# One loop for the score and value products, weights per unit, one eviction per block, in an attention kernel on one core

## The chip, the core and the metric

The kernel runs on one core of a Trainium2 chip. The core has five engines that run side by side, each with its own instruction stream: TensorE (PE in the profile; its weight loads are listed apart, as PEld), VectorE (DVE), ScalarE (ACT), GpSimd (POOL) and SyncE (SP), which here only issues transfers. Transfers between the main memory (DRAM) and the on-chip memory (SBUF) run on 16 DMA engines; matrix products go to the accumulator memory (PSUM). The engines wait for each other on semaphores. The metric is the device time of one execution in microseconds (us), lower is better.

## What is computed

Attention for 128 heads (8 batches of 16) with 16 queries per head, 2048 keys, head size 256, all bf16:

```python
B, H, Sq, Skv, Dh = 8, 16, 16, 2048, 256
def reference(q, k, v):
    scale = q.shape[-1] ** -0.5
    scores = jnp.einsum('bhqd,bhkd->bhqk', q, k) * scale
    attn = _softmax(scores, axis=-1)
    return jnp.einsum('bhqk,bhkd->bhqd', attn, v)
```

K and V are 134 MB each and every byte is read once; q and the output are 1 MB each.

## The kernel before

**Units and blocks.** The 128 heads are cut into 16 blocks of 8 heads (`g`, 0 to 15, `last` is 15), each block into two units of 4 heads (`e`, 0 and 1). K or V of one unit is 4.19 MB and fills one of four SBUF slots of `SL`: `KA` and `KB` for K of unit 0 and 1, `VA` and `VB` for V. K of block 0 goes to the V slots instead (`kslot`, L93), so that K of block 1 can be loaded at once. K(g,e) and V(g,e) stand below for these transfers. A partition holds 64 consecutive rows (`T`) of the unit; t counts them.

**One block on the engines.** VectorE transposes K of a unit in place, in 32x32 squares of 4-byte words, in four instructions of 16 rows each (L154); each pair of them releases one half `h` of the unit's scores (`c_kt[e][h]`). TensorE then makes the scores of both units into four PSUM banks `S_ps` (`qk`, L239 to L247): for each of 8 weight sets, 2 products per half, one weight load for each pair (L233 leaves the load out for the second). The last product of a unit adds to `c_qk[e]`. VectorE takes the negated row maximum (L156), ScalarE the exponentials with their sums in two halves (L206), VectorE transposes them into `PTc` (L162), and ScalarE copies them with eight instructions into `PTz` (L219), the zero-padded weights of the second product. TensorE multiplies `PTz` with V, 64 rows t per unit, 128 products with 128 weight loads per block (`pv`, L249, L251), into one PSUM bank per unit (`obank`). ScalarE evicts each unit's rows with the factor 1/sum into `O_fin` (L180) and issues the store (L184); the products of block g-1 come behind the scores of block g, and so do their eviction and store (`finish`).

**TensorE's order.** Scores of block 0; then a loop over g = 1 to 15 of scores of g and products of g-1 (L266 to L274); then the products of block 15 written out, with their own weights (`z` = 1), their own two banks and a wait for each piece of V(15,0) (`TAIL_A`) and V(15,1) (`TAIL`, pieces of 19 down to 2 rows).

**Transfers.** SyncE issues all loads from one queue, in a fixed order, and a wait in it holds up all behind it (L99 to L134): q, K(0,0), K(0,1), then for each g K(g,0), K(g,1), V(g-1,0), V(g-1,1). K(g,e) waits for the scores that used the slot (`c_qk[e]`), V(g-1,e) for the products that used it (`c_pv[e]`). At the end V(15,0) and V(15,1) go to the K slots and wait for the scores of block 15 (L126 to L131). K(15,1) and V(14,1) are loaded in two halves, with a semaphore for each.

**ScalarE's order.** For block g: the next block's query weights (L174), the exponentials, then `finish(g-1)`, which waits for all products of g-1, and only then the eight copies into `PTz`, since one set of weights serves all blocks but the last.

Of the kernel before, what the change touches and what calls it, by code (L numbers as in the profile page):

```python
# [9 lines left out]
F32 = mybir.dt.float32  # L10
# [5 lines left out]
def bass_standalone__softmax_full_bidir__sampling_kernel(  # L16
# [20 lines left out]
    with ExitStack() as es:  # L37
# [5 lines left out]
        PTc = ec(nc.sbuf_tensor("PTc", [128, T, 32], BF16))  # L43
        PTz = ec(nc.sbuf_tensor("PTz", [128, 2, T, 128], BF16))
        O_fin = ec(nc.sbuf_tensor("O_fin", [128, 2, D], BF16))
# [6 lines left out]
        O_ps = ec(nc.psum_tensor("O_ps", [128, 4, 512], F32))  # L52
# [8 lines left out]
        s_st = [sem("s_st%d" % i) for i in range(2)]  # L61
# [12 lines left out]
        c_pl = sem("c_pl")  # L74
# [8 lines left out]
        TAIL = [(0, 19), (19, 14), (33, 10), (43, 7), (50, 5), (55, 4), (59, 3), (62, 2)]  # L83
        TAIL_A = [(0, 37), (37, 27)]
        s_tail = [sem("s_t%d" % i) for i in range(len(TAIL))]
        s_vl = [sem("s_vl%d" % i) for i in range(len(TAIL_A))]
        s_vc = sem("s_vc")
        s_kl = sem("s_kl")

        def obank(g, e):  # L90
            return e + (2 if g == last else 0)
# [7 lines left out]
        def on_sync(eng):  # L99
            eng.dma_start(QT[:], qh).then_inc(s_q, 16)  # L100
            for e in range(2):
                load(eng, ku, 0, e, kslot(0, e), 0, T, s_k0[e])
            for g in range(1, G):
                for e in range(2):
                    if g >= 2:
                        eng.wait_ge(c_qk[e], g)
                    if (g, e) != (last, 1):
                        load(eng, ku, g, e, kslot(g, e), 0, T, s_k[e])
                    else:
                        load(eng, ku, g, e, kslot(g, e), 0, 32, s_k[e])  # L110
                        load(eng, ku, g, e, kslot(g, e), 32, 32, s_kl)
                w = g - 1
                for e in range(2):
                    if w:
                        eng.wait_ge(c_pv[e], w)
                    else:
                        eng.wait_ge(c_qk[e], 1)
                    if (w, e) != (last - 1, 1):
                        load(eng, vu, w, e, (VA, VB)[e], 0, T, s_v[e])
                        if e:  # L120
                            eng.sem_inc(s_vc, 16)
                    else:
                        load(eng, vu, w, e, VB, 0, 32, s_v[e])
                        load(eng, vu, w, e, VB, 32, 32, s_vc)
# [7 lines left out]
            eng.wait_ge(c_ev, 2 * last + 2)  # L132
            eng.dma_start(oh[128 * last:128 * last + 128, :], O_fin[:, last % 2, :]).then_inc(s_fin, 16)
            eng.wait_ge(s_fin, 16)  # L134
# [4 lines left out]
        def on_vector(eng):  # L139
# [4 lines left out]
            for g in range(G):  # L144
                for e in range(2):
                    for c in range(4):
                        if g == 0 and c == 0:
                            eng.wait_ge(s_k0[e], 16)
                        elif c == 0:
                            eng.wait_ge(s_k[e], 16 * g)  # L150
                        elif (g, e, c) == (last, 1, 2):
                            eng.wait_ge(s_kl, 16)
                        x = SLf[:, kslot(g, e), 16 * c:16 * c + 16, :].rearrange("p t i -> p (t i)")
                        eng.transpose(x, x).then_inc(c_kt[e][c // 2], 1)  # L154
# [13 lines left out]
        def on_scalar(eng):  # L168
# [9 lines left out]
            def evac(g, e):  # L178
                rows = slice(64 * e, 64 * e + 64)
                eng.activation(O_fin[rows, g % 2, :], O_ps[rows, obank(g, e), 0:D],  # L180
                               ACTF.Copy, scale=rinv[rows, g:g + 1]).then_inc(c_ev, 1)

            def store(g):
                eng.dma_start(oh[128 * g:128 * g + 128, :], O_fin[:, g % 2, :]).then_inc(s_st[g % 2], 16)  # L184

            def finish(g):
                eng.wait_ge(c_ri, 2 * g + 2)
                if g >= 2:
                    eng.wait_ge(s_st[g % 2], 16 * (g // 2))
                for e in range(2):  # L190
                    eng.wait_ge(c_pv[e], g + 1)
                    evac(g, e)
                eng.wait_ge(c_ev, 2 * g + 2)
                store(g)
# [3 lines left out]
            for g in range(G):  # L198
                if g < last:
                    eng.wait_ge(c_qk[1], g + 1)  # L200
                    qwb(g + 1)
                eng.wait_ge(c_mx, g + 1)
                if g:
                    eng.wait_ge(c_pt, 2 * g)
# [9 lines left out]
                z = 1 if g == last else 0  # L214
                for e in range(2):
                    for a in range(4):
                        rs = 32 * (2 * e + a // 2)
                        sv = PTc[rs:rs + 32, :, :]
                        eng.activation(PTz[32 * a:32 * a + 32, z, :, 64 * e + 16 * a:64 * e + 16 * a + 16],  # L219
                                       sv[:, :, 16 * (a % 2):16 * (a % 2) + 16], ACTF.Copy).then_inc(c_cp, 1)  # L220
            finish(last - 1)
            eng.wait_ge(c_ri, 2 * G)
            eng.wait_ge(s_st[last % 2], 16 * (last // 2))
            eng.wait_ge(c_pl, 1)
            evac(last, 0)
            eng.wait_ge(c_pl, 2)
            evac(last, 1)
            eng.wait_ge(s_st[0], 16 * (G // 2))

        def on_tensor(eng):  # L230
# [8 lines left out]
            def qk(g, e, h, slot):  # L239
                kb0 = SL[:, slot, 0, :]  # L240
                for bp in range(8):
                    b, par = bp // 2, bp % 2
                    for c in (2 * h, 2 * h + 1):
                        ins = mm(S_ps[:, c, :], QW[:, e, :, bp],
                                 ap_of(kb0, kb0.offset + 16 * c * D + 64 * b + par, [[D, 16], [2, 32]]),
                                 e == 0 and bp == 0, e == 1 and bp == 7, c % 2 == 0)
                return ins  # L247

            def pv(e, slot, z, bank, t0, t1):  # L249
                for t in range(t0, t1):  # L250
                    ins = eng.matmul(O_ps[:, bank, 0:D], PTz[:, z, t, :], SL[:, slot, t, :],  # L251
                                     start=(t == 0), stop=(t == T - 1))
                return ins

            def qks(g):
                for e in range(2):
                    for h in range(2):
                        eng.wait_ge(c_kt[e][h], 2 * g + 2)
                        if e == 0 and h == 0 and not (isinstance(g, int) and g == 0):
                            eng.wait_ge(c_ex[1], g)  # L260
                        ins = qk(g, e, h, kslot(0, e) if isinstance(g, int) and g == 0 else (KA, KB)[e])
                    ins.then_inc(c_qk[e], 1)

            eng.wait_ge(c_qw, 4)
            qks(0)
            with nc.Fori(1, G, engines=[PE], head_slot={PE: 0}) as g:  # L266
                qks(g)
                eng.wait_ge(c_cp, 8 * g)
                for e in range(2):
                    eng.wait_ge(s_v[e], 16 * g)  # L270
                    if e:
                        pv(e, VB, 0, e, 0, 32)
                        eng.wait_ge(s_vc, 16 * g)
                    pv(e, (VA, VB)[e], 0, e, 32 * e, T).then_inc(c_pv[e], 1)  # L274
            eng.wait_ge(c_cp, 8 * G)
            for (a, n), s in zip(TAIL_A, s_vl):
                eng.wait_ge(s, 16)
                ins = pv(0, KA, 1, obank(last, 0), a, a + n)
            ins.then_inc(c_pl, 1)
            for (a, n), s in zip(TAIL, s_tail):  # L280
                eng.wait_ge(s, 16)
                ins = pv(1, KB, 1, obank(last, 1), a, a + n)
            ins.then_inc(c_pl, 1)
# [34 lines left out]
```

## Time and profile before

| | us |
|---|---|
| median of 3 runs (lowest to highest) | 636.06 (636.02 to 636.25) |
| the profiled execution | 636.1 |
| its span, first to last instruction | 634.8 |
| TensorE products busy | 488.3 |
| VectorE busy | 365.2 |
| ScalarE busy | 214.8 |

Busy times of different engines overlap. In the profile a row such as `L154 DVE STREAM_TRANSPOSE SL<-SL` names the line of the kernel, the engine, the operation, and the tile written and read. A row of the timeline has the start and the length in us; several like instructions are merged (x8), and square brackets give the engine's idle time before them and what ended it. SPq and ACTq are the issue of a transfer, not the transfer; how long one takes from issue to landing is told in rows of their own, with its size in KB.

### The profile page before, as it was taken

The page shows a single profiled execution, that of the slowest core. Times are in us where ns is not written, and L with a number is a line of the kernel's source. Part 1 is how long each engine was busy: PE and PEld are TensorE (multiplying, and loading weights), DVE is VectorE, ACT ScalarE, POOL GpSimd, SP SyncE. Part 2 cuts the span into 40 slices and gives each one's busy share as a digit, 9 for nine tenths or more (in the row PEclk, how much of TensorE's full clock was granted, in tenths as well). Part 3 has the DMA queues.
Part 4 walks back from the last instruction along what each step waited for, and adds up shares of the span by engine and source line. Part 5 has one row for each costly group of instructions (what it writes and reads, how often), then busy time and mean ns, then how long its engine had stood idle before and what let it go on. Part 6 is the DMA issues. An engine that isn't in the chain of part 4 may idle for free.

```text
span 634.8 us, 6396 instructions
## 1 busy us (share of the span) xinstructions
PE 488.3 (77%) x3072; PEld 274.9 (43%) x2560; DVE 365.2 (58%) x210; ACT 214.8 (34%) x289; POOL 7.1 (1%) x5
## 2 busy tenths in 40 slices
PE   0738989595896958869597795967959689595998
PEld 0202828154271532716336262452724527144287
DVE  2968583763738546294562945739366393663830
ACT  1042252525035250342513325142252322524170
POOL 4000000000000000000000000000000000000000
PEclk9978999798997989969799797998979989798899
DMA  8999999999999999999999999999999999999997
GB/s 376 436 441 432 428 432 432 430 430 431 432 429 434 429 432 433 429 434 429 433 430 429 432 429 433 430 430 433 434 429 436 433 433 432 432 432 425 430 425 285
DMA packets 13113, 270.64 MB, mean 426 GB/s; under 512 B 1456, under 2 KB 3760, under 8 KB 4400
## 3 DMA queue, kind: packets, MB, share of 16 engines
q1 hardware_dynamic: 10944, 269.55, 98.8%
q10 hardware_dynamic: 2160, 0.98, 0.5%
q8 instruction: 3, 0.05, 0.0%
q14 instruction: 6, 0.05, 0.0%
HBM read 269.48 MB, written 1.05 MB: 426 GB/s over the span
## 4 chain that ended last, share of the span: by engine, by line
DMA 58%; PE 23%; DVE 16%; ACT 2%; issue 0%; SPq 0%
DMA SL<-in_k_dram 58%; DVE SL L154 15%; PE S_ps L234 11%; PE S_ps L235 10%; PE O_ps L251 2%; ACT PTz L219 1%; DVE PTc L162 1%; DVE negm L156 1%; ACT P_sb L206 0%; ACT O_fin L180 0%; SPq L97 0%; SPq L100 0%; DVE rinv L166 0%; DVE ltot L164 0%
## 5 line engine op out<-in xcount | busy, mean ns | idle before, releaser
L154 DVE STREAM_TRANSPOSE SL<-SL 128x2048 f32<-128x2048 f32 x128 | 284.2, 2279 | 157.9 <-DMA SL<-in_k_dram 157.9
L234 PE MATMUL S_ps<-SL,QW 128*128 128x512 bf16 x512 | 214.0, 418 | 143.5 <-DVE SL L154 143.3
L251 PE MATMUL O_ps<-SL,PTz 128*128 128x256 bf16 x2048 | 226.3, 273 | 0.9 <-ACT PTz L219 0.7
L234 PEld LDWEIGHTS S_ps<-SL,QW 128*128 128x128 bf16 x512 | 75.1, 147 | 326.6 <-issue 171.7
L251 PEld LDWEIGHTS O_ps<-SL,PTz 128*128 128x128 bf16 x2048 | 199.8, 98 | 30.9 <-issue 4.5
L235 PE MATMUL S_ps<-SL,QW 128*128 128x512 bf16 x512 | 212.5, 415 | 0.0
L219 ACT ACTIVATE PTz<-PTc 32x1024 bf16<-32x1024 bf16 x128 | 134.9, 1054 | 11.3 <-ACT O_fin L180 5.9
L174 ACT ACTIVATE QW<-QT 32x256 bf16<-32x256 bf16 x64 | 26.8, 419 | 243.3 <-PE S_ps L235 236.2
L156 DVE TENSOR_REDUCE negm<-S_ps 128x1 f32<-128x2048 f32 x16 | 36.7, 2292 | 61.4 <-PE S_ps L235 61.4
L180 ACT ACTIVATE O_fin<-O_ps,rinv 64x256 bf16<-64x256 f32 x32 | 15.0, 468 | 137.6 <-PE O_ps L251 137.5
L162 DVE STREAM_TRANSPOSE PTc<-P_sb 128x1024 bf16<-128x1024 bf16 x32 | 37.9, 1224 | 20.3 <-ACT P_sb L206 20.3
L206 ACT ACTIVATE P_sb<-S_ps,negm 128x1024 bf16<-128x1024 f32 x32 | 35.3, 1109 | 25.5 <-DVE negm L156 25.5
L137 POOL MEMSET PTz<- 128x8192 f32 x1 | 6.9, 6924 | 0.3 <-POOLq L303 0.3
L206 ACT ACTIVATION_READ_ACCUMULATOR P_sb<-S_ps,negm 128x1 f32 x32 | 6.3, 196 | 0.0
L143 DVE STREAM_TRANSPOSE QT<-QT 128x2048 f32<-128x2048 f32 x1 | 2.3, 2312 | 3.7 <-DMA QT<-in_q_dram 3.7
L166 DVE RECIPROCAL rinv<-ltot 128x1 f32<-128x1 f32 x16 | 2.6, 164 | 0.5
L164 DVE TENSOR_REDUCE ltot<-lsum 128x1 f32<-128x2 f32 x16 | 1.8, 112 | 0.0
L174 ACT ACT_TABLE_LOAD x1 | 1.3, 1283 | 0.7 <-PEq L303 0.7
L140 DVE MEMSET QW<- 128x1024 f32 x1 | 0.9, 912 | 1.0 <-PEq L303 1.0
L303 POOL MEMSET const-bfloat16-1.0<- 128x1 bf16 x1 | 0.1, 101 | 0.0
L303 POOL MEMSET const-uint8-127<- 128x1 uint8 x1 | 0.1, 101 | 0.0
L303 POOL MEMSET const-float32-0.0<- 128x1 f32 x1 | 0.1, 98 | 0.2 <-issue 0.2
(1 smaller groups left out, 0.1 us busy)
## 6 DMA issues: line engine op xcount, KB each, us to landing
SL<-in_k_dram SPq DMA_DIRECT2D x31, 4096.0 KB, 25.8
SL<-in_v_dram SPq DMA_DIRECT2D x29, 4096.0 KB, 29.1
SL<-in_k_dram SPq DMA_DIRECT2D x2, 2048.0 KB, 23.7
SL<-in_v_dram SPq DMA_DIRECT2D x2, 2048.0 KB, 29.2
SL<-in_v_dram SPq DMA_DIRECT2D x1, 2368.0 KB, 21.6
SL<-in_v_dram SPq DMA_DIRECT2D x1, 1728.0 KB, 25.4
SL<-in_v_dram SPq DMA_DIRECT2D x1, 1216.0 KB, 20.7
QT<-in_q_dram SPq DMA_DIRECT2D x1, 1024.0 KB, 4.9
```

Source lines behind the costliest of these rows:

```text
L137: eng.memset(PTz[:].rearrange("p a t c -> p (a t c)").bitcast(F32), 0.0).then_inc(c_pool, 1)
L154: eng.transpose(x, x).then_inc(c_kt[e][c // 2], 1)
L156: eng.tensor_reduce(out=negm[:, g:g + 1], in_=S_ps[:].rearrange("p c n -> p (c n)"), axis=AX.X, op=ALU.max, negate=True).then_inc(c_mx, 1)
L162: eng.transpose(PTc[:, 32 * h:32 * h + 32, :].rearrange("p t x -> p (t x)"), P_sb[:, 1024 * h:1024 * h + 1024]).then_inc(c_pt, 1)
L166: eng.reciprocal(rinv[:, g:g + 1], ltot[:, g:g + 1]).then_inc(c_ri, 1)
L174: eng.activation(ap_of(dv, dv.offset, [[1024 + 512, 2], [2, 64], [1, 2]]), ap_of(sv, sv.offset + 2 * (8 * r + a), [[8, 2], [64, 64], [1, 2]]),
L180: eng.activation(O_fin[rows, g % 2, :], O_ps[rows, obank(g, e), 0:D], ACTF.Copy, scale=rinv[rows, g:g + 1]).then_inc(c_ev, 1)
L206: eng.activation(P_sb[:, 1024 * h:1024 * h + 1024], S_ps[:, 2 * h:2 * h + 2, :].rearrange("p c n -> p (c n)"), ACTF.Exp, bias=negm[:, g:g ...
L219: eng.activation(PTz[32 * a:32 * a + 32, z, :, 64 * e + 16 * a:64 * e + 16 * a + 16], sv[:, :, 16 * (a % 2):16 * (a % 2) + 16], ACTF.Copy) ...
L234: return eng.matmul(dst, w, x, start=start, stop=stop)
L235: return eng.add_instruction(mybir.InstMatmult(name=nc.get_next_instruction_name(), engine=PE, start_tensor_calc=start, stop_tensor_calc=stop,
L251: ins = eng.matmul(O_ps[:, bank, 0:D], PTz[:, z, t, :], SL[:, slot, t, :], start=(t == 0), stop=(t == T - 1))
```

## The change

TensorE's code outside the loop shrinks to the scores of block 0, which now wait for the whole transposed unit and take the four banks with one weight load for each of the 8 weight sets. The loop runs 16 passes, r = 1 to 16: scores of block r if r is below 16, then the products of block r-1, the last block's too. The piecewise waits for V stand in every pass, against a limit that is 1 up to the pass where the piece's own semaphore is really used; SyncE adds 1 to these semaphores once, at g = 1, to `c_ev` as well.

`PTz`'s two sets are now one per unit: copies of unit 0 fill set 0, columns 0 to 63, and those of unit 1 fill set 1, columns 64 to 127. All 128 products of a block add into one PSUM bank, which one instruction evicts. The first product of a block waits for the eviction of the block before (`c_ev`). Copies of unit 0 wait for unit 0's products of the block before, then comes that block's eviction and store, then the copies of unit 1. `O_fin` has a place for each block, and the waits for a free place go.

V of block 15 is loaded into `VA` and `VB`, behind the products of block 14, in the same pieces as before. K(15,0) is loaded in halves as K(15,1) was. V(14,1) is cut at row 33 instead of 32. VectorE transposes 32 rows per instruction instead of 16.

```diff
+        PIECES = [[(0, 37), (37, 27)],
+                  [(0, 19), (19, 14), (33, 10), (43, 7), (50, 5), (55, 4), (59, 3), (62, 2)]]
+        MID = 33
...
-                    if (g, e) != (last, 1):
+                    if g < last:
                         load(eng, ku, g, e, kslot(g, e), 0, T, s_k[e])
                     else:
                         load(eng, ku, g, e, kslot(g, e), 0, 32, s_k[e])
-                        load(eng, ku, g, e, kslot(g, e), 32, 32, s_kl)
...
-            eng.wait_ge(c_qk[0], G)
-            for (a, n), s in zip(TAIL_A, s_vl):
-                load(eng, vu, last, 0, KA, a, n, s)
-            eng.wait_ge(c_qk[1], G)
-            for (a, n), s in zip(TAIL, s_tail):
-                load(eng, vu, last, 1, KB, a, n, s)
+                        load(eng, ku, g, e, kslot(g, e), 32, 32, s_kl[e])
+                if g == 1:
+                    for x in [c_ev] + list(s_p[0].values()) + list(s_p[1].values()):
+                        eng.sem_inc(x, 1)
+                for w in ((g - 1,) if g < last else (g - 1, g)):
+                    for e in range(2):
+                        if w:
+                            eng.wait_ge(c_pv[e], w)
...
+                        pieces = [(0, T)]
+                        if w == last:
+                            pieces = PIECES[e]
+                        elif (w, e) == (last - 1, 1):
+                            pieces = [(0, MID), (MID, T - MID)]
+                        for a, n in pieces:
+                            load(eng, vu, w, e, (VA, VB)[e], a, n, s_p[e][a] if a else s_v[e])
...
-                    for c in range(4):
...
-                        x = SLf[:, kslot(g, e), 16 * c:16 * c + 16, :].rearrange("p t i -> p (t i)")
-                        eng.transpose(x, x).then_inc(c_kt[e][c // 2], 1)
+                    for h in range(2):
+                        if h == 0:
+                            eng.wait_ge(s_k[e] if g else s_k0[e], 16 * max(g, 1))
+                        elif g == last:
+                            eng.wait_ge(s_kl[e], 16)
+                        x = SLf[:, kslot(g, e), 32 * h:32 * h + 32, :].rearrange("p t i -> p (t i)")
+                        eng.transpose(x, x).then_inc(c_kt[e][h], 1)
...
+            def evac(g):
+                eng.wait_ge(c_pv[1], g + 1)
+                if g == last:
+                    eng.wait_ge(c_ri, 2 * G)
+                eng.activation(O_fin[:, g, :], O_ps[:, 0:D], ACTF.Copy, scale=rinv[:, g:g + 1]).then_inc(c_ev, 1)
+
+            def copies(e):
+                for a in range(4):
+                    rs = 32 * (2 * e + a // 2)
+                    sv = PTc[rs:rs + 32, :, :]
+                    m = 64 * e + 16 * a
+                    eng.activation(PTz[32 * a:32 * a + 32, e, :, m:m + 16],
+                                   sv[:, :, 16 * (a % 2):16 * (a % 2) + 16], ACTF.Copy).then_inc(c_cp, 1)
...
-                if 0 < g < last:
-                    finish(g - 1)
...
                 eng.wait_ge(c_pt, 2 * g + 2)
...
+                if g:
+                    eng.wait_ge(c_pv[0], g)
+                copies(0)
+                if g:
+                    evac(g - 1)
+                    eng.wait_ge(c_ev, g + 1)
+                    eng.dma_start(oh[128 * (g - 1):128 * g, :], O_fin[:, g - 1, :]).then_inc(s_st, 16)
+                copies(1)
+            evac(last)
...
+            eng.wait_ge(c_qw, 4)
+            for e in range(2):
+                eng.wait_ge(c_kt[e][1], 1)
+                qk(e, (0, 1, 2, 3), kslot(0, e)).then_inc(c_qk[e], 1)
+
+            with nc.Fori(1, G + 1, engines=[PE]) as r:
+                with eng.If_lt(eng.to_reg(r), G):
+                    for e in range(2):
+                        for h in range(2):
+                            eng.wait_ge(c_kt[e][h], r + 1)
+                            if e == 0 and h == 0:
+                                eng.wait_ge(c_ex[1], r)
+                            ins = qk(e, (2 * h, 2 * h + 1), (KA, KB)[e])
+                        ins.then_inc(c_qk[e], 1)
+                lim1 = (r & 16) + 1
+                lim2 = lim1 + ((r + 1) & 16)
                 for e in range(2):
...
+                    if e == 0:
+                        eng.wait_ge(c_ev, r)
+                    eng.wait_ge(c_cp, 8 * r - 4 + 4 * e)
+                    eng.wait_ge(s_v[e], 16 * r)
+                    for t in range(T):
+                        if t in s_p[e]:
+                            eng.wait_ge(s_p[e][t], lim2 if (e, t) == (1, MID) else lim1)
+                        ins = eng.matmul(O_ps[:, 0:D], PTz[:, e, t, :], SL[:, (VA, VB)[e], t, :],
+                                         start=(e == 0 and t == 0), stop=(e == 1 and t == T - 1))
+                    ins.then_inc(c_pv[e], 1)
```

More of the change, by code (lines that the diff above doesn't have):

```diff
@@ L60, in bass_standalone__softmax_full_bidir__sampling_kernel @@
         s_v = [sem("s_va"), sem("s_vb")]
-        s_st = [sem("s_st%d" % i) for i in range(2)]
+        s_st = sem("s_st")
         s_fin = sem("s_fin")
@@ L73, in bass_standalone__softmax_full_bidir__sampling_kernel @@
         c_pv = [sem("c_pv0"), sem("c_pv1")]
-        c_pl = sem("c_pl")
         c_ev = sem("c_ev")
@@ L80, in ap_of @@
             return bass.AP(tensor=t_ap.tensor, offset=offset, ap=[list(t_ap.ap[0])] + [list(d) for d in dims])
[L83 to L91, printed above, removed]
+        PIECES = [[(0, 37), (37, 27)],
+                  [(0, 19), (19, 14), (33, 10), (43, 7), (50, 5), (55, 4), (59, 3), (62, 2)]]
+        MID = 33
+        s_p = [{a: sem("s_p%d_%d" % (e, a)) for a, n in PIECES[e][1:]} for e in range(2)]
+        s_kl = [sem("s_kl%d" % e) for e in range(2)]
         def kslot(g, e):
@@ L176, in qwb @@
                                    ACTF.Copy, scale=scale).then_inc(c_qw, 1)
[L178 to L194, printed above, removed]
+            def evac(g):
[10 more added lines that the diff above has]
+                                   sv[:, :, 16 * (a % 2):16 * (a % 2) + 16], ACTF.Copy).then_inc(c_cp, 1)
             eng.wait_ge(c_qt, 2)
@@ L213, in on_scalar @@
                 eng.wait_ge(c_pt, 2 * g + 2)
[L214 to L228, printed above, removed]
+                if g:
[7 more added lines that the diff above has]
+            evac(last)
+            eng.wait_ge(s_st, 16 * last)
         def on_tensor(eng):
@@ L237, in mm, with qk @@
                     ldweights=False, ins=[eng.lower_ap(x), eng.lower_ap(w, for_matmul_weights=True)], outs=[eng.lower_ap(dst)]))
-            def qk(g, e, h, slot):
+            def qk(e, cs, slot):
                 kb0 = SL[:, slot, 0, :]
@@ L242, in qk @@
                     b, par = bp // 2, bp % 2
-                    for c in (2 * h, 2 * h + 1):
+                    for c in cs:
                         ins = mm(S_ps[:, c, :], QW[:, e, :, bp],
                                  ap_of(kb0, kb0.offset + 16 * c * D + 64 * b + par, [[D, 16], [2, 32]]),
-                                 e == 0 and bp == 0, e == 1 and bp == 7, c % 2 == 0)
+                                 e == 0 and bp == 0, e == 1 and bp == 7, c == cs[0])
                 return ins
[L249 to L253, printed above, removed]
@@ L255, in qks @@
-            def qks(g):
-                for e in range(2):
[L257 to L278, printed above, removed]
```

36 lines of the change are left out of this document (6 added, 30 removed).

## The prediction, made before the changed kernel had run

> **What bounds the kernel now.** I read the page first, its parts 1 to 3: which engine is full?
>
> ```profile
> span 634.8 us, 6396 instructions
> PE 488.3 (77%) x3072; PEld 274.9 (43%) x2560; DVE 365.2 (58%) x210; ACT 214.8 (34%) x289; POOL 7.1 (1%) x5
> DMA  8999999999999999999999999999999999999997
> q1 hardware_dynamic: 10944, 269.55, 98.8%
> q8 instruction: 3, 0.05, 0.0%
> ```
>
> No compute engine is full; the 16 DMA engines are, in every slice but the first and the last. The table by stretches of time says how full (last columns: granted clock, DMA share, GB/s):
>
> ```profile
> 48.00:87.00 39.00, 36.98 (x223) 19.48 (x176) 29.57 (x18) 15.86 (x22) 0.00 (x0) 0.96 1.00 430
> 611.00:628.00 17.00, 16.31 (x150) 14.37 (x149) 0.00 (x0) 8.73 (x10) 0.00 (x0) 1.00 0.99 415
> 629.00:630.00 1.00, 1.00 (x11) 0.89 (x10) 0.00 (x0) 0.00 (x0) 0.00 (x0) 1.00 0.56 197
> 630.00:631.00 1.00, 1.00 (x12) 0.90 (x10) 0.00 (x0) 0.00 (x0) 0.00 (x0) 1.00 0.33 119
> 631.00:632.00 1.00, 1.00 (x12) 0.90 (x10) 0.00 (x0) 0.00 (x0) 0.00 (x0) 1.00 0.04 14
> ```
>
> One block of 39 us moves four 4.19 MB transfers, 16.8 MB / 39.0 us = 430 GB/s. As long as a transfer always stands in the queue, nothing that an engine saves inside a block shortens the run. So the two ends decide. The chain of waits, its last pieces (start, us, what):
>
> ```profile
> 557.59 24.80 DMA SL<-in_k_dram
> 582.41 17.67 DVE SL L154 x8
> ...
> 617.42 1.06 ACT PTz L219
> 618.53 14.16 PE O_ps L251 x128
> 632.71 0.47 ACT O_fin L180
> ```
>
> Here the end is a chain of compute: K of block 15 lands at 582.4, eight transposes run without a gap, then scores, softmax, eight copies, and only at 618.53 the 128 products of block 15. Were they waiting for V? The sync engine's issues (start, us), and behind them the same five transfers with KB and us from issue to landing:
>
> ```profile
> 572.96 0.33 SPq L97 DMA_DIRECT2D SL<-in_v_dram  x1
> 580.33 0.42 SPq L97 DMA_DIRECT2D SL<-in_v_dram  x1
> 595.88 0.33 SPq L97 DMA_DIRECT2D SL<-in_v_dram  x1
> 596.25 0.43 SPq L97 DMA_DIRECT2D SL<-in_v_dram  x1
> 613.00 3.94 SPq L97 DMA_DIRECT2D SL<-in_v_dram  x1
> ```
> ```profile
> SL<-in_v_dram SPq DMA_DIRECT2D x1, 4096.0 KB, 29.1
> SL<-in_v_dram SPq DMA_DIRECT2D x1, 2048.0 KB, 31.5
> SL<-in_v_dram SPq DMA_DIRECT2D x1, 2368.0 KB, 21.6
> SL<-in_v_dram SPq DMA_DIRECT2D x1, 1728.0 KB, 25.4
> SL<-in_v_dram SPq DMA_DIRECT2D x1, 128.0 KB, 18.8
> ```
>
> Landings: V(14,0) 602.1, V(14,1) 611.8, V(15,0) 617.5 and 621.7, the last piece of V(15,1) 613.0 + 18.8 = 631.8. The last product starts at about 632.4 (618.53 + 14.16 less its own 0.27). So compute ends the run, but the data is only some 0.5 us behind it: that is all a better order of the tail can win.
>
> **The change, part by part.**
>
> *Tail, K(15,0) in halves.* Its first half now has its own semaphore. The halves of K(15,1) show what a half is worth:
>
> ```profile
> 565.97 0.33 SPq L97 DMA_DIRECT2D SL<-in_k_dram  x1
> 566.34 0.44 SPq L97 DMA_DIRECT2D SL<-in_k_dram  x1
> ```
> ```profile
> SL<-in_k_dram SPq DMA_DIRECT2D x1, 2048.0 KB, 21.4
> SL<-in_k_dram SPq DMA_DIRECT2D x1, 2048.0 KB, 26.0
> ```
> ```profile
> 582.41 17.66 DVE L154 STREAM_TRANSPOSE SL<-SL 128x2048 f32<-128x2048 f32 x8 [10.26 <-DMA SL<-in_k_dram]
> ```
>
> They land at 587.4 and 592.3, so half of K(15,0) is there at about 577.4, in the 10.3 us in which VectorE idles. Two old transposes (2 x 17.66 / 8 = 4.4 us) become one. VectorE then follows the landings: 577.4 to 581.8, 582.4 to 586.8, 587.4 to 591.8, 592.3 to 596.7, where it ended at 600.1. The scores end 3.4 us earlier, at about 600.5 instead of 603.9. Doubling the transposes can save at most a start-up per pair and is hidden by the landings; I take nothing.
>
> *Tail, V(15) goes to VA and VB.* V(15,0) waited for scores (595.88); now it waits for the products of V(14,0). Those start when V(14,0) lands, 602.1 (scores end before it). From the first product of a block to the V issue behind its first half:
>
> ```profile
> 565.78 14.13 PE L251 MATMUL O_ps<-SL,PTz 128*128 128x256 bf16 x128
> ```
>
> 572.96 - 565.78 = 7.2 us, so V(15,0) is issued at 609.3. Behind it on the sync engine stands only V(15,1), which gets its slot at 602.1 + 14.2 = 616.3. How long from an issue to first bytes? The last store shows it:
>
> ```profile
> 633.21 0.35 SPq L133 DMA_DIRECT2D out_dram<-O_fin  x1
> ```
> ```profile
> 633.00:633.80 0.80, 0.00 (x0) 0.00 (x0) 0.00 (x0) 0.18 (x1) 0.00 (x0) 1.00 0.00 0
> 633.80:634.40 0.60, 0.00 (x0) 0.00 (x0) 0.00 (x0) 0.00 (x0) 0.00 (x0) 1.00 0.38 109
> ```
>
> 0.6 to 1.2 us; with 0.9 the bytes of V(15,0) arrive at 610.2, 1.6 us before V(14,1) has landed on the slowest engine. The engines do not finish together: in the last stretches above the share falls over 2.4 us, so some may idle before 610.2. Lower bound of the gap: 0. Upper: the whole fall, 0.44 + 0.67 + 0.96 = 2.1 us. With bytes arriving 1.6 us before the last landing only the first part of the fall is exposed; I take 0.1 us. V(15,1) at 616.3 is 5 us ahead of V(15,0)'s last landing: no gap.
>
> *Tail, one bank, one eviction, weights per unit.* The products of block 15 now wait for the eviction of block 14 (one O bank): it starts when PE is done at 616.3, takes 0.47, so PE goes on at 616.9. Copies(0) of block 15 run when the products of V(14,0) free their half (609.3 to 613.6), copies(1) behind eviction and store issue, 617.2 to 621.5; unit 1's products need them at 624. PE runs unit 0 from 616.9, waits at t=37 for 621.7, is through at 624.7, and from there follows the pieces of V(15,1) to 631.8. Two products, then the eviction: 632.2 instead of 632.7. The tail gains 0.5 us. PE can be 1 us later at 616.9 before that gain shrinks.
>
> *Head.* Block 0's scores wait for whole transposes, and four chunks share one weight load.
>
> ```profile
> 25.05 8.89 DVE L154 STREAM_TRANSPOSE SL<-SL 128x2048 f32<-128x2048 f32 x4 [0.82 <-DMA SL<-in_k_dram]
> 37.78 0.33 SPq L97 DMA_DIRECT2D SL<-in_v_dram  x1
> 56.96 0.33 SPq L97 DMA_DIRECT2D SL<-in_k_dram  x1
> ```
> ```profile
> SL<-in_k_dram SPq DMA_DIRECT2D x1, 4096.0 KB, 17.8
> ```
>
> Unit 1's transposes end at 33.9, and its scores at 37.8, when V(0,1) is issued: 3.8 us for the last 16 products. Now all 32 come after 33.9, so block 0 ends about 3.7 us later. Unit 0's lie under unit 1's transposes, as before; V(0,0) may come later behind them, since K(0,1) has landed at 25.05 and the two K of block 1 hold the DMA for 2 x 9.75 us more, to 44.5. The first load that feels the delay is K(2,0), issued at 60.7 instead of 56.96. It landed at 74.8; 39 / 4 = 9.75 us of transfer and the 0.9 us of start mean that 64.1 would still do: 3.4 us of cover are left, and beyond them each us late is a us of run. Cost 0.
>
> *Loop, per block.* TensorE gets an if, some register arithmetic and about eight more waits. The ten waits in the old tail cost nothing (14.16 for 128 products there, 14.13 in the loop). Branch and arithmetic have no row; a sync issue (0.33 us) is the nearest, so 0 to 14 x 0.33 = 4.6 us per block. Cover: TensorE's idle stretch before the scores:
>
> ```profile
> 586.97 0.65 PE L234 MATMUL S_ps<-SL,QW 128*128 128x512 bf16 x1 [7.05 <-DVE SL L154]
> ```
>
> 7.05 us in every block; so 0 in the stream, and in the tail the 1 us of slack. ScalarE's half as many evictions, the dropped waits on PT and stores, and sync's ten semaphore steps (all while two or more transfers are queued) lie beside the DMA: 0.
>
> **Sum.** Span 634.8 - 0.5 (tail) + 0.1 (handover) = 634.4; the profiled execution took 636.1, 1.3 beyond its span, and the median is 636.06: 635.7 us. A measurement of this kernel tells about 0.2% (1.3 us) from no change, so this is no change.
>
> **The rivals.**
>
> A, slower: *the handover starves DMA.* V(15) loses its early issue. If the scores of block 15 end as late as before, products start at 603.7, V(15,0) is issued at 610.9 and its bytes come at 611.8, when V(14,1) has landed: the whole fall, 2.1 us, and 636.06 - 0.5 + 2.1 = 637.7. It decides from 1.9 us of gap, an issue after about 610.8. Against it: VectorE is idle for 10.3 us before 582.41.
>
> B, slower: *the loop's top in the tail.* Block 15's products come from a 16th pass, so the branch round the scores and the arithmetic stand between 616.3 and the first product. Up to 4.6 us less 1 of slack, half of it likelier: 637.0 to 639.3. For it: the trace of before holds no forward branch that is taken, so nothing bounds it from nearer. Against: the c_ev wait (616.3 to 616.9) runs at the same time.
>
> C, slower: *instruction fetch.* A back-edge that fetched code through the same full queues could take as long as a 64 KB store under load; at 14 us (such stores' median, below) it exceeds the 7.05 us of cover by 7 us in each of 15 passes, some 740 us in all.
>
> ```profile
> out_dram<-O_fin ACTq DMA_DIRECT2D x15, 64.0 KB, 14.0
> ```
>
> Against it: the old loop too has 3072 / 16 + 2560 / 16 = 352 instructions of array work in a pass, and the q8 row counts 3 instruction packets in the whole run, so passes did not refetch. [...]
>
> D, no change at all: *the tail stays a compute tail* because copies or eviction come later than I put them: 636.1.
>
> E, faster: *the last pieces land sooner.* If the DMA kept 430 instead of 415 GB/s from 611 to 628, 17 x (1 - 415 / 430) = 0.6 us: 635.1. More than 1.3 us would need something I do not see.
>
> **How the numbers follow.** Forecast 0.60 (its own range 635.0 to 636.6), A 0.16, B 0.10, C 0.03, D 0.06, E 0.05. Faster by over 0.2% (below 634.8): most of E and a little of the forecast's edge, 0.06. Slower (above 637.3): A, B, C and an edge of 0.02, 0.31. Within: 0.63. The range reaches from E to the middle of B: 634.8 to 638.2, with C and B's far end left out.
>
> **What would show it.** DMA share 1.00 and some 430 GB/s in every stretch from 48 to 594; K(15)'s transposes start near 577.4 and scores end near 600.5; V(15,0) issued near 609.3, and no dip of GB/s between 609 and 613; products of block 15 start near 617 and end within 0.5 us of the last landing near 631.8. Wrong: a dip there (A), a stretch without products behind the eviction of block 14 (B), more q8 packets (C), or K(2,0) landing after 74.8 (head).

## The result, and the profile after

| | before | after |
|---|---|---|
| median, us (lowest to highest, runs) | 636.08 (635.79 to 636.25, 8) | 638.18 (637.35 to 639.11, 8) |
| the profiled execution, its span | 636.1, 634.8 | 637.77, 636.4 |

The changed kernel is slower: 1.0034 times the time before, interval 1.0023 to 1.0045. The forecast was 635.7 and no change; 638.18 lies at the very top of the range, where the slower rivals had 0.31. Two later sessions with the same kernel gave 636.85 (1.0018 [1.0006, 1.0030]) and 636.67 (1.0012 [1.0003, 1.0021]). So the loss is 0.7 to 2.1 us by the medians, and single runs spread over 4 us (635.5 to 639.7), where the kernel before spreads over 1.0 (635.66 to 636.62). Both facts need a cause.

Parts 1 and 3 of the page of the kernel after (engines with busy time; DMA queues with packets, MB and share):

```profile
span 636.4 us, 6411 instructions
PE 489.3 (77%) x3072; PEld 271.0 (43%) x2544; DVE 361.7 (57%) x146; ACT 207.4 (33%) x273; POOL 7.1 (1%) x5
q1 hardware_dynamic: 11088, 269.55, 98.7%
q8 instruction: 2, 0.03, 0.0%
```

The work shrank as the diff says (DVE 210 to 146 instructions, ACT 289 to 273), TensorE's products are as many, and two packets in the q8 row, in a run of 16 passes, say that the longer loop does not fetch its code again in each pass. The end of the chain of waits (start, us, what):

```profile
573.01 29.26 DMA SL<-in_v_dram
602.32 7.17 PE O_ps L251 x64
609.51 0.33 SPq L94
609.88 12.54 DMA SL<-in_v_dram
622.46 10.61 PE O_ps L251 x91
633.09 0.47 ACT O_fin L173
```

Before, the chain ended in 128 products and a softmax. Now it ends in a transfer, and that transfer hangs on a sync issue at 609.51 which waits for 64 products. The timeline of the kernel after, cut to the tail's landmarks:

```profile
577.75 4.45 DVE L145 STREAM_TRANSPOSE SL<-SL 128x4096 f32<-128x4096 f32 x1 [5.55 <-DMA SL<-in_k_dram]
600.84 2.29 DVE L147 TENSOR_REDUCE negm<-S_ps 128x1 f32<-128x2048 f32 x1 [3.83 <-PE S_ps L213]
616.50 0.47 ACT L173 ACTIVATE O_fin<-O_ps,rinv 128x256 bf16<-128x256 f32 x1 [2.63 <-PE O_ps L251]
618.19 14.86 PE L251 MATMUL O_ps<-SL,PTz 128*128 128x256 bf16 x128 [1.73 <-DMA SL<-in_v_dram]
633.09 0.47 ACT L173 ACTIVATE O_fin<-O_ps,rinv 128x256 bf16<-128x256 f32 x1 [11.41 <-PE O_ps L251]
633.59 0.35 SPq L126 DMA_DIRECT2D out_dram<-O_fin  x1
```

The compute of the tail came as forecast, within 0.4 us at each landmark (577.4, 600.5, 616.3). But the products of block 15 start at 618.19 behind the landing of V(15,0), with 1.73 us of idle, and the last eviction comes at 633.09 instead of 632.71. The issues of K(2,0) and of the last piece, and the transfers of K(2,0), of V(15,0)'s first piece, of the last piece and of the last store (KB, us to landing):

```profile
60.49 0.33 SPq L94 DMA_DIRECT2D SL<-in_k_dram  x1
619.86 0.46 SPq L94 DMA_DIRECT2D SL<-in_v_dram  x1
```
```profile
SL<-in_k_dram SPq DMA_DIRECT2D x1, 4096.0 KB, 15.1
SL<-in_v_dram SPq DMA_DIRECT2D x1, 2368.0 KB, 8.6
SL<-in_v_dram SPq DMA_DIRECT2D x1, 128.0 KB, 12.7
out_dram<-O_fin SPq DMA_DIRECT2D x1, 64.0 KB, 2.8
```

The last store of the kernel before took:

```profile
out_dram<-O_fin SPq DMA_DIRECT2D x1, 64.0 KB, 1.5
```

The data's end is 619.86 + 12.7 = 632.6, where it was 631.8; the store takes 2.8 instead of 1.5. So the span's +1.6 us is +0.4 at the eviction (the data are 0.8 later, but compute is no longer the 0.5 behind them) and some +1.25 in the last store.

**Where the data's 0.8 us went.** The table by stretches of the kernel after (second number the stretch's length; last columns granted clock, DMA share, GB/s):

```profile
63.00:64.00 1.00, 1.00 (x5) 0.14 (x1) 1.00 (x1) 0.00 (x0) 0.00 (x0) 1.00 1.08 361
64.00:65.00 1.00, 0.42 (x3) 0.22 (x2) 0.58 (x1) 0.00 (x0) 0.00 (x0) 1.00 1.05 360
...
609.00:610.00 1.00, 1.00 (x12) 0.90 (x10) 0.00 (x0) 0.43 (x1) 0.00 (x0) 1.00 0.63 270
610.00:611.00 1.00, 1.00 (x12) 0.90 (x10) 0.00 (x0) 0.98 (x2) 0.00 (x0) 1.00 1.39 370
611.00:612.00 1.00, 1.00 (x12) 0.90 (x10) 0.00 (x0) 0.98 (x2) 0.00 (x0) 1.00 0.44 152
612.00:613.00 1.00, 1.00 (x11) 0.90 (x10) 0.00 (x0) 0.97 (x2) 0.00 (x0) 1.00 1.13 474
```

and the same view of the kernel before:

```profile
63.00:64.00 1.00, 1.00 (x6) 0.29 (x2) 0.00 (x0) 0.00 (x0) 0.00 (x0) 1.00 1.22 524
64.00:65.00 1.00, 1.00 (x6) 0.36 (x3) 0.00 (x0) 0.00 (x0) 0.00 (x0) 1.00 1.22 524
...
609.00:610.00 1.00, 1.00 (x11) 0.90 (x10) 0.97 (x3) 0.13 (x1) 0.00 (x0) 1.00 0.94 399
610.00:611.00 1.00, 1.00 (x11) 0.90 (x10) 0.07 (x1) 0.98 (x2) 0.00 (x0) 1.00 1.16 496
611.00:612.00 1.00, 1.00 (x12) 0.89 (x10) 0.00 (x0) 1.00 (x1) 0.00 (x0) 1.00 0.98 417
```

Two dips: 361 and 360 GB/s at 63 to 65, where K(2,0) follows V(0,1), and 152 to 370 at 609 to 612, where V(15,0) follows V(14,1). (The view counts a packet whole in the stretch in which it starts, so a share can pass 1 and a single us is only rough.) The transfer records don't name the engine, but in the middle of the run 16 packets are under way at any time. What is missing to 16, in us and as the mean of the 16 DMA engines, is the idle:

```
idle, us              60-70   70-607  607-613
before                0       0       0
after                 0.25    0       0.52
after, session 2      0.15    0       1.59
after, session 3      0.07    0       0.55
```

0.25 + 0.52 = 0.77 is close to the 0.8 by which the last piece lands late. The match is not exact: in sessions 2 and 3 the sums are 1.74 and 0.62, and the last piece lands 1.39 and 0.29 later than before. Hence three suspects: the head, the handover at 609, and the last store.

### The profile page after: what moved, and what is told of

Same layout as the page of the kernel before. It is cut to its first block, busy times and chain, and to the rows that moved or that the text cites. A ratio compares the mean times of both kernels' runs of the same rounds, so it can differ in the third digit from the quotient of the medians.

```text
span 636.4 us, 6411 instructions
## 1 busy us (share of the span) xinstructions
PE 489.3 (77%) x3072; PEld 271.0 (43%) x2544; DVE 361.7 (57%) x146; ACT 207.4 (33%) x273; POOL 7.1 (1%) x5
## 4 chain that ended last, share of the span: by engine, by line
DMA 63%; DVE 23%; PE 13%; ACT 0%; issue 0%; SPq 0%
DMA SL<-in_k_dram 56%; DVE SL L145 22%; DMA SL<-in_v_dram 7%; PE S_ps L213 5%; PE S_ps L212 5%; PE O_ps L251 4%; DVE PTc L153 0%; DVE negm L147 0%; ACT P_sb L191 0%; SPq L94 0%; ACT O_fin L173 0%; SPq L97 0%; DVE rinv L157 0%; DVE ltot L155 0%
## 5 line engine op out<-in xcount | busy, mean ns | idle before, releaser
L145 DVE STREAM_TRANSPOSE SL<-SL 128x4096 f32<-128x4096 f32 x64 | 280.8, 4424 | 154.8 <-DMA SL<-in_k_dram 154.8
L212 PE MATMUL S_ps<-SL,QW 128*128 128x512 bf16 x496 | 206.6, 417 | 140.3 <-DVE SL L145 140.2
L251 PE MATMUL O_ps<-SL,PTz 128*128 128x256 bf16 x2048 | 228.6, 273 | 3.4 <-DMA SL<-in_v_dram 3.2
L213 PE MATMUL S_ps<-SL,QW 128*128 128x512 bf16 x528 | 213.2, 414 | 0.0
L212 PEld LDWEIGHTS S_ps<-SL,QW 128*128 128x128 bf16 x496 | 72.6, 146 | 324.5 <-issue 177.7
L173 ACT ACTIVATE O_fin<-O_ps,rinv 128x256 bf16<-128x256 f32 x16 | 7.6, 474 | 52.8 <-PE O_ps L251 52.8
```

What stands on the lines that cost most here:

```text
L145: eng.transpose(x, x).then_inc(c_kt[e][h], 1)
L173: eng.activation(O_fin[:, g, :], O_ps[:, 0:D], ACTF.Copy, scale=rinv[:, g:g + 1]).then_inc(c_ev, 1)
L212: return eng.matmul(dst, w, x, start=start, stop=stop)
L213: return eng.add_instruction(mybir.InstMatmult(name=nc.get_next_instruction_name(), engine=PE, start_tensor_calc=start, stop_tensor_calc=stop,
L251: ins = eng.matmul(O_ps[:, 0:D], PTz[:, e, t, :], SL[:, (VA, VB)[e], t, :], start=(e == 0 and t == 0), stop=(e == 1 and t == T - 1))
```

## The experiments

"Before" is here the kernel before in the same session, with medians from 635.91 to 636.03.

**Undoing one thing of the changed kernel.** First the place of the loop in TensorE's code, set to slot 0 as in the kernel before:

```diff
-            with nc.Fori(1, G + 1, engines=[PE]) as r:
+            with nc.Fori(1, G + 1, engines=[PE], head_slot={PE: 0}) as r:
```

> The changed kernel with one edit: the loop's first instruction is placed at the start of a fetch page, as in the kernel before. Theory F (a fetch of an instruction page when TensorE leaves the loop, 634.05 to 635.38 in the changed kernel's trace, holds up one DMA engine's share of the final store): no instruction packet of q8 after 600, the final store lands 1.5 us after its issue instead of 2.8, and the time falls by about 1.2 us, to some 637.0. Rival (the final store is slower for another reason, such as its larger O_fin buffer or the loop's exit itself): q8 moves or not, the store still takes 2.8 us, and the time stays near 638.2.

637.44 us (636.30 to 639.33), 1.0026 [1.0014, 1.0037]. Its last store took 1.5 us, as theory F has it, but the time fell by 0.7 and not by 1.2. What the expectations call a fetch page shows in the traces as an instruction packet of 16 KB (`q8`); where in the code one begins is not shown. It ran again beside the changed kernel itself:

> The changed kernel unchanged, for a comparison on one chip with the next three: 638.2 as before (637.4 to 639.1), a q8 packet at about 634 and the final store landing 2.8 us after its issue.

> The changed kernel with the loop at the start of a fetch page, again (637.44 in 7 runs from 636.3 to 639.3). Theory F (the page fetch at the loop's exit costs the final store 1.2 us): 1.2 us below the unchanged one in the same session, and no execution's final store is late. If the first difference of 0.7 was chance: the two agree.

636.85 and 636.56 (before 635.93), with runs from 635.5 to 639.7 in both: 0.3 apart and not 1.2, not to be told from each other. So what makes the medians is not mainly the loop's place. In this profile of the changed kernel the last store took 1.5 us too; the 2.8 comes and goes.

Then the head, block 0's scores in halves as before:

```diff
-                eng.wait_ge(c_kt[e][1], 1)
-                qk(e, (0, 1, 2, 3), kslot(0, e)).then_inc(c_qk[e], 1)
+                for h in range(2):
+                    eng.wait_ge(c_kt[e][h], 1)
+                    ins = qk(e, (2 * h, 2 * h + 1), kslot(0, e))
+                ins.then_inc(c_qk[e], 1)
```

> The changed kernel with block 0's scores in halves again, each with its own weight loads, as before (16 more instructions ahead of the loop). Head theory: K(2,0) is issued at about 57 instead of 60.5, no DMA engine idles at 63 to 64, which is worth 0.25 us. [...]

636.14 us (635.25 to 636.96), 1.0001 [0.9992, 1.0010]: the loss is gone, where the 0.25 expected for the head would have left 637.9. The idle at 60 to 70 is 0.01 now; at 607 to 613 there is still 0.76. Both edits at once:

> The changed kernel with both edits, block 0's scores in halves and the loop at the start of a fetch page; against the run with the page edit alone (637.44, from 636.3 to 639.3) only the head differs. Head theory: the 3.5 us later issue of K(2,0) costs what this run gains, about 1.3 us in the median, although that run's profile shows an idle of only 0.1 us at 63; the time is near 636.1. If the gap between the page run and the halves run came from where the loop stands, this one stays at 637.4.

635.90 us (635.54 to 637.46), 1.0003 [0.9994, 1.0012]: with the place held, the head alone takes 637.44 and 636.56 down to 635.90, and against 636.14 the place adds nothing that can be seen in the median. Three of the 11 runs took 637.3 to 637.5 all the same, and the one with the profile, 637.46, shows a cause that is neither head nor handover: no idle at 60 to 70, 0.74 at 607 to 613, but a granted clock of 0.50 in the stretches from 619 to 622. The 128 last products took 15.8 us instead of 14.9, and the last eviction came at 634.06, 1.4 us behind the last landing (632.62) instead of 0.5.

**Doing one part alone in the kernel before.** K(15,0) in halves, with a semaphore each, and nothing else:

```diff
-                    if (g, e) != (last, 1):
+                    if g != last:
...
-                        load(eng, ku, g, e, kslot(g, e), 32, 32, s_kl)
+                        load(eng, ku, g, e, kslot(g, e), 32, 32, s_kl[e])
```

> The kernel before with one edit: K(15,0) is loaded and transposed in halves, with a semaphore for the second. My sum for the tail: the scores of block 15 end at 600.5 instead of 603.9, products of block 15 start at 616.4 instead of 618.5 and end with the last landing, so the time falls by 0.5 us, to 635.6. Rival: the end hangs on the last landing alone, 636.1.

635.75 us, 0.9995 [0.9986, 1.0004]; 0.28 below before by the medians. In its chain of waits the products of block 15 start at 617.59 (expected 616.4) and the eviction at 632.29, 0.42 earlier:

```profile
617.59 14.67 PE O_ps L251 x128
632.29 0.47 ACT O_fin L180
```

So the forecast's tail gain of 0.5 is there by the trace, and with it the data set the end: the last piece lands at 631.81, as before. Now the handover is added: V(15,0) and V(15,1) keep their slots, but wait for the products of block 14 as in the changed kernel.

```diff
             eng.wait_ge(c_qk[0], G)
+            eng.wait_ge(c_pv[0], last)
...
             eng.wait_ge(c_qk[1], G)
+            eng.wait_ge(c_pv[1], last)
```

> The same with a second edit: the loads of V(15,0) and V(15,1) also wait for the products of V(14,0) and V(14,1), as in the changed kernel; slots, loop and tail are those of before. Handover theory: V(15,0) is issued at 609.5 instead of 592.5, DMA engines idle about 0.5 us (mean of the 16) between 609.3 and 611.1, and the last landing comes 0.5 us later than in the kernel with halves alone: some 0.5 us slower than that one. If the handover costs nothing, both have the same time; if it explained the whole slowdown, this one would be 2 us slower.

637.17 us, 1.0017 [1.0008, 1.0026]: 1.42 above the one without, nearly three times the 0.5 expected. The last landing moved from 631.81 to 633.39, the eviction from 632.29 to 633.87. Its stretches:

```profile
609.00:610.00 1.00, 1.00 (x12) 0.90 (x10) 0.00 (x0) 0.97 (x2) 0.00 (x0) 1.00 0.31 131
610.00:611.00 1.00, 1.00 (x12) 0.90 (x10) 0.00 (x0) 1.00 (x1) 0.00 (x0) 1.00 1.22 307
611.00:612.00 1.00, 1.00 (x11) 0.90 (x10) 0.00 (x0) 0.98 (x2) 0.00 (x0) 1.00 0.61 227
```

The same dip as in the changed kernel, made by the added waits; the mean idle of the engines is 0.89 us here and 0.00 without them. Then the head alone: block 0's scores of a unit after both its halves, four chunks per weight load.

```diff
-            qks(0)
+            for e in range(2):
+                eng.wait_ge(c_kt[e][1], 2)
+                for bp in range(8):
...
+                    for c in range(4):
+                        ins = mm(S_ps[:, c, :], QW[:, e, :, bp],
...
+                ins.then_inc(c_qk[e], 1)
```

> The kernel before with one edit: block 0's scores wait for the whole unit and take four chunks per weight load, as in the changed kernel. Head theory: K(2,0) is issued 3.5 us later, at 60.5; some DMA engines idle at 63 to 64 in some executions, and up to 1.3 us are lost in the median, less what the end of this kernel hides (0.5 us): 636.1 to 636.9, with a wider spread than 635.8 to 636.2. If the head costs nothing: 636.0.

636.89 us (635.83 to 639.3), 1.0022 [1.0011, 1.0033]: one edit in the old kernel costs 0.98 by the median and brings the wide spread with it. K(2,0) is issued at 60.92 instead of 56.96, and in its stretches the dip at 63 to 65 appears (426 and 360 against 524 and 524 GB/s) while 609 to 612 stays full:

```profile
63.00:64.00 1.00, 1.00 (x6) 0.28 (x2) 1.00 (x1) 0.00 (x0) 0.00 (x0) 1.00 1.33 426
64.00:65.00 1.00, 0.46 (x3) 0.05 (x1) 0.90 (x1) 0.00 (x0) 0.00 (x0) 1.00 0.94 360
...
609.00:610.00 1.00, 1.00 (x12) 0.90 (x10) 1.00 (x2) 0.00 (x0) 0.00 (x0) 1.00 1.05 446
610.00:611.00 1.00, 1.00 (x11) 0.90 (x10) 0.48 (x3) 0.68 (x1) 0.00 (x0) 1.00 1.01 432
611.00:612.00 1.00, 1.00 (x11) 0.90 (x10) 0.00 (x0) 0.98 (x2) 0.00 (x0) 1.00 1.01 433
```

**Curing the handover instead.** In the changed kernel the product of row 36, the last of V(15,0)'s first piece, releases that piece's slot at once:

```diff
+                        if (e, t) == (0, 36):
+                            ins.then_inc(c_pm, 1)
...
-                        if w:
+                        if (w, e) == (last, 0):
+                            eng.wait_ge(c_pm, w)
+                        elif w:
                             eng.wait_ge(c_pv[e], w)
...
+                            if a and (w, e) == (last, 0):
+                                eng.wait_ge(c_pv[0], w)
```

With the head in halves as well:

> The changed kernel with block 0's scores in halves, and the first piece of V(15,0), rows 0 to 36, released as soon as those rows of V(14,0) are used, by a semaphore of its own at product 36. Handover theory: that piece is issued at about 606.5 instead of 609.4, no DMA engine idles between 607 and 613 (0.76 us in the halves run), and the time falls by about 0.8 us to 635.3, below the kernel before (636.03). If the handover is not what is left, the time stays at 636.1.

635.45 us (635.27 to 635.71), 0.9993 [0.9984, 1.0002]; all 11 runs lie below the lowest of the 33 of before in that session (635.74). Then a square of both edits on one chip, before at 635.98:

> First corner of a square on one chip: the changed kernel itself. Two sessions gave 638.18 and 636.85 in the median, from 635.5 to 639.7; between 636.8 and 638.2 again, with a standard deviation over 0.5.

> Second corner: block 0's scores in halves. Head theory: 1 to 2 us below the first corner, near 636.1; if the head is not a cause, as the first corner.

> Third corner, not run so far: the early release of V(15,0)'s first piece alone, the head as in the changed kernel. If head and handover are two causes that add up, 0.5 to 0.7 us below the first corner, with its wide spread, since the head stays: 636.3 to 637.5. If the handover is where the head's late engines are paid for, the spread closes too and the time is near the fourth corner, 635.5.

> Fourth corner: both edits. 635.45 again, below the kernel before by some 0.5 us, standard deviation under 0.2.

| | scores of block 0 whole | in halves |
|---|---|---|
| V(15,0) issued behind 64 products | 636.67, 1.0012 [1.0003, 1.0021] | 635.88, 1.0001 [0.9993, 1.0010] |
| behind 37 products | 636.08, 1.0007 [0.9998, 1.0016] | 635.59, 0.9993 [0.9984, 1.0002] |

By the medians the head is worth 0.79, the handover 0.59 in the left column and 0.29 in the right, both together 1.08. Only the 0.79 and the 1.08 stand clear of the spread: single runs reach from 635.97 to 637.43, 635.47 to 638.85, 635.51 to 637.51 and 635.16 to 636.00 in the four corners, so whether the two add up (1.38) stays open. The third corner came below the 636.3 expected and kept the wide spread; only the fourth is narrow. The chain of waits of the kernel with both ends so:

```profile
601.79 4.23 PE O_ps L258 x37
606.04 11.14 DMA SL<-in_v_dram
617.23 14.80 PE O_ps L258 x128
632.05 0.47 ACT O_fin L178
```

V(15,0) is issued at 606.04, 3.0 us earlier than in the second corner (609.01), and its stretches have no dip:

```profile
609.00:610.00 1.00, 1.00 (x12) 0.89 (x10) 0.00 (x0) 0.95 (x1) 0.00 (x0) 1.00 1.01 430
610.00:611.00 1.00, 1.00 (x12) 0.90 (x10) 0.00 (x0) 0.98 (x2) 0.00 (x0) 1.00 1.00 430
611.00:612.00 1.00, 1.00 (x12) 0.90 (x10) 0.00 (x0) 0.97 (x2) 0.00 (x0) 1.00 0.98 417
```

**The last store.** In the window 632 to 637 of the kernel after the DMA queues are:

```profile
q1 hardware_dynamic: 153, 0.07, 5.3%
q8 instruction: 1, 0.02, 1.7%
```

One instruction packet stands beside the store; 1.7% of 16 x 5 us is 1.4 us of one DMA engine. By the records it ends at 635.38; 15 of the 16 engines have completed the store by 634.79; the last one's share starts as the packet ends and is through at 635.81. The kernel with the early release alone shows the same a second time, in the same window:

```profile
q8 instruction: 1, 0.02, 1.3%
...
out_dram<-O_fin SPq DMA_DIRECT2D x1, 64.0 KB, 2.6
```

In all other profiles the store took 1.5 or 1.6, with no such packet beside it. Can it be called up by the place of the loop? Three kernels, each the one with the head in halves and a loop that starts at another slot (138, 144, 145; the choice was the author's estimate, and no run shows that a fetch depends on it):

> [...] Theory F: a q8 packet at about 634, the final store lands 2.7 instead of 1.5 us after its issue, and the time is about 1.2 us above the halves run (636.14), near 637.3. If the fetch is harmless: 636.1.

> [...] Theory F: a q8 packet at about 634, the final store lands 2.7 us after its issue, and the time is 1.2 us above the run with slot 138 (636.02), near 637.2. [...]

> [...]

636.02 (1.0008 [0.9998, 1.0017]), 636.02 (1.0008 [0.9999, 1.0017]) and 637.20 (1.0021 [1.0011, 1.0031]). None of the three profiles has a packet at the end, so the test missed: whatever decides that fetch, it was not called up in the profiled executions.

An effect of the place is on record all the same, in the time of each run less its span. It is 1.26 to 1.40 us in all 135 runs of the kernel before, in all 28 of the changed loop at slot 0, in all 45 with the head in halves and no slot set, and in all 33 of the edited old kernels. In the changed kernel (three sessions), the one with the early release alone and the three with slots 138, 144 and 145 it is 1.47 to 2.50 us in 21 of 73 runs; the median run of slot 145, 637.20, has a span of 634.7. So a part of what these kernels lose lies outside the span, where the profile has no row. What happens there is not shown.

## Why the prediction failed, point by point

**What bounds the kernel: right.** The stretches of 39 us between 87 and 594 have 431 to 433 GB/s before and after; no saving inside a block shortened the run. The one from 48 to 87, with the head's dip in it, fell from 430 to 421.

**The tail's compute: right, in mechanism and nearly in size.** The transposes, scores, issue and eviction came at 577.75, 600.84, 609.51 and 616.50, forecast 577.4, 600.5, 609.3 and 616.3. Alone in the kernel before, K(15,0) in halves brought 0.42 in the trace and 0.28 in the median, against 0.5.

**"Cost 0" of the head: wrong, the first of two failed steps.** The prediction said "64.1 would still do: 3.4 us of cover are left". Its own sign of being wrong came: K(2,0) landed at 60.49 + 15.1 = 75.6, after 74.8. The step took one landing, 74.8, for all engines, and 0.9 us from issue to first bytes from a store of 64 KB. First and last of the 16 engines' completions, from the records:

```
us                      before              after
V(0,1) ends             63.02 to 64.61      62.81 to 63.40
K(2,0) issued           56.96               60.49
K(2,0) ends             72.73 to 74.32      72.99 to 75.08
V(14,1) ends            608.97 to 611.33    609.20 to 611.57
```

A landing follows the completion of the last engine (75.6 behind 75.08 for K(2,0)); before, the others were through with V(0,1) up to 1.6 us sooner, from 63.0 on. And this transfer did not reach all engines in 0.9 us: after the issue at 60.49, 11 engines had K(2,0)'s packets by the time V(0,1) ended there, and 5 got them only between 63.6 and 64.4, up to 3.9 us behind the issue (2.0 to 3.9 over the profiles with these scores whole). By this estimate the queue had at worst to be fed by 63.0 - 3.9 = 59.1, which is 2.2 us of cover; the issue moved by 3.5. In the median the head costs 0.8 (square) to 1.0 (alone in the kernel before). The profiles show at most 0.26 of idle for it. What the runs above 638 lose, up to 639.7, is not shown: none of them has a trace. It need not be the head, since with the head in halves single runs still reach 638.85.

**"I take 0.1 us" for the handover: wrong, the second.** The bounds, 0 to 2.1, held it; the choice did not. It set bytes at 610.2 against a last landing at 611.8, although the prediction had itself seen that "the engines do not finish together". 14 engines were through with V(14,1) between 609.2 and 610.9, and V(15,0)'s first packets came from 610.47 on, on the last idle engine at 611.14, 1.6 us behind the issue: 0.52 us of mean idle, 1.59 in another profile. The median cost is 0.3 (the square's right column, hardly clear of the spread) to 1.4 (the waits alone in the kernel before). Why it differs so much stays open. That is rival A's mechanism, *the handover starves DMA*, with the dip it asked for, in the order of 0.5 to 1 us instead of 2.1, and with the issue at 609.5, well ahead of the 610.8 from which A was to decide. The mean idle is not the cost: a landing follows the last engine (75.6 behind 75.08 above). In the second corner's profile 0.59 of idle left the last piece where it was (631.76, before 631.81), while 0.26 at the head of the old kernel moved it by 0.5 (632.33).

**The last store: never costed.** The sum took "1.3 beyond its span" and the old store as they were. In two of the four profiles with block 0's scores whole and the loop at its place (three of the changed kernel, one with the early release) it took 1.1 to 1.3 us longer, beside an instruction packet. How often this happens in runs without a profile stays open, and so does why the medians of three sessions differ (638.18, 636.85, 636.67). The time outside the span, a constant 1.3 in the sum too, was 1.47 to 2.18 in 9 of the 31 runs of these sessions.

**The loop: right inside the span.** Rival B's stretch without products is there (616.97 to 618.19), but it waits for V(15,0), as its bracket says; with the early release the products start at 617.23 with the same loop. The sum had these products start at 616.9, although its own landing of V(15,0)'s first piece was 617.5. Rival C's fetch in every pass did not happen: two `q8` packets in 16 passes, and no idle of the DMA engines from 70 to 607. The one at the end cost something all the same: the last store beside it took 1.1 to 1.3 us longer. The prediction argued against C from the old loop's trace; for the longer loop only its own trace shows it, and what sets off a fetch is not shown.

**The version that keeps the gain** has the changed loop, block 0's scores in halves and the early release: 635.45 and 635.59 in two sessions, some 0.4 us below before in both, though each interval still reaches 1.0002. Its 22 runs lie between 635.16 and 636.00.

## What to carry to other kernels

Where the DMA stream is the bound, a later issue has to be priced at the moment when the first engine's queue runs dry, and with the time until the last of the 16 engines has packets of a transfer of that size (here 63.0 and up to 3.9 us), not with one landing time and the first byte of a small store (74.8 and 0.9). A buffer that is refilled in pieces should be released in pieces: one semaphore on the 37th of 64 products brought the issue 3.0 us forward and closed the gap. A median close to the old one is no proof of an untouched kernel: with one end still open, single runs reached 637.5, 638.9 and 639.3 at medians of 636.08, 635.88 and 636.89, and the version with both ends cured stayed within 0.9 us. The spread alone doesn't name its cause, though: a traced run at 637.46 lost 1.0 us of it to the granted clock, and some others lost up to 1.2 us outside the span.

## What the runs showed of the hardware

- The five 16 KB instruction packets in the traces of before and after took 0.92 to 1.33 us each. In the kernel before, one at 37.6 us came as the engines' spread at the end of a transfer went from 0.35 us (K(1,0)) to 1.6 (K(1,1)): the last engine ended 1.25 us behind the one next to last there, still 1.27 behind at V(0,0) and at V(0,1). The spread is 2.4 at V(14,1). In the kernel after, whose first such packet comes at 68.8, the spread is still 0.6 at V(0,1) and 2.1 at K(2,0).
- From issue to the packets on the last idle engine: 2.0 to 3.9 us for the 4.19 MB of K(2,0) in a queue still busy, 1.2 to 2.1 for the first 2.4 MB piece of V(15,0), and 1.2 at most for the 64 KB store in an empty queue.
- The last store landed 2.8 and 2.6 us after its issue in the two profiles with a packet beside it (the changed kernel, the early release alone), 1.5 or 1.6 in all others; in the changed kernel one of three profiles had the packet.
